# A gated long convolution and an MLP on one core: two causal half-length transforms in a fixed engine order, in place of one padded transform and a scheduled MLP

## The chip, the cores and the metric

The kernel runs on one core of one Trainium2 chip. The metric is device time in microseconds (us), lower is better. TensorE (PE) does the matmuls, VectorE (DVE) and ScalarE (ACT) move accumulated sums out of PSUM (below: evictions) and do the elementwise work, GpSimd (POOL) does small vector work, and SyncE (SP) issues most DMAs. A run has a state: the profiled ones here are fast unless it is said otherwise, and only fast runs enter a ratio.

## The reference, cut to what matters

The sizes are S=2048 positions, D=512 channels and F=1792 hidden channels, in bfloat16.

```python
h  = x + q' * (conv(kv, ssm_k) + kv * ssm_D)     # x = A_q, q' = layernorm(x)
     # kv = (4-tap shift convolution of k) * v
     # conv: rfft over 4096 points (zero padded), product, irfft, first 2048 kept
h2 = h + mlp(layernorm(h))                       # the output
     # g  = gelu(layernorm(.) @ w1); channel quarters shifted by -1, +1, -2, +2 positions
     # x1 = . + g @ w2
     # x1 + gelu(layernorm(x1) @ w3) @ w4
```

The convolution is causal: output half 1 (positions 1024 to 2047) needs input half 1, but output half 0 doesn't. The MLP needs only a few neighbouring positions. So the MLP of half 0 could begin before the convolution of half 1 is done.

## The kernel before

One padded 4096-point transform is written as matmuls in two steps with an exchange by DMA between them. This is done for the filter and for kv. Then come the spectrum products, two inverse steps with a second exchange between them, and then the MLP. Filter and k are brought into their layouts on the chip:

```python
nc.sync.dma_start(hnat[:, c, :], A_ssm_k[c * P:(c + 1) * P, :])
nc.sync.dma_start_transpose(kT[:, c, 16:KW], k_r[:, c * P:(c + 1) * P])
...
nc.tensor.transpose(pt[:, j, :], hnat[:, c, 8 * bh + j:S:16], ident[:])   # 64 of these
...
def step2(z, kh, name):                       # 32 groups of 4 matmuls, 128 x 64
    for r in range(2):
        for t in range(2):
            nc.tensor.matmul(ps[64 * t:64 * t + 64, r, :], lhsT=ftab[:, kh, r, t, :], rhs=z[:, kh, t, :], ...)
...
for i in range(NH + 2):                       # products and inverse, whole sequence
    if i < NH:
        prs[i] = fwd(i)                       # step 2 of kv, eviction on ACT, 2 products on DVE
    if i >= 2:
        inv(i - 2, prs[i - 2])                # 8 matmuls, eviction, DMA exchange
...
plan = Plan({"mm": 6, "pt": 2, "lb": 6, "z": 4})   # from here on: gating, norms and MLP, put in
...                                                # order by a priority search when the kernel is built
for b in range(NB):
    task(("Y", b), {"A": 0.72}, gate(b), ...)
    task(("H", b), {"V": 1.6}, hsum(b), ...)
```

The list of tasks that the search may interleave begins only behind the whole convolution, with the last inverse step.

## Time and profile before

| | before |
|---|---|
| time, median of 3 runs (range) | 268.09 us (267.1 to 268.8) |
| span of the profiled run | 266.8 us |
| PE, DVE, ACT, POOL busy | 231.9, 161.9, 143.3, 54.1 us |
| first w3 matmul | 157 us |

These lines of the page give busy time by engine, and the span in 40 slices of 6.7 us. A digit is the busy share of a slice in tenths, and PEclk is the granted TensorE clock in tenths.

```profile
PE 231.9 (87%) x1803; PEld 119.0 (45%) x1803; DVE 161.9 (61%) x323; ACT 143.3 (54%) x202; POOL 54.1 (20%) x101
...
PE   8665957999579988665988999999999999999994
...
DVE  7986807669927998299999994898022250013322
...
PEclk9999995999959999796899999999999999999999
...
PE 57%; DVE 24%; DMA 6%; ACT 5%; POOL 4%; issue 2%; ACTq 0%; POOLq 0%
```

PE is busy for 87% of the span, but its digits of 9 stand together only from slice 22 on (slices are counted from 0; this one begins at 147 us). Before it they lie between 5 and 9. The last line is the chain of work that ended last, by engine: DVE and DMA hold 30% of it, and that is where PE had to wait.

The same kernel by stage follows: the window, its length, busy time of each engine (with the number of instructions), granted clock, DMA share, GB/s.

```profile
0.00:60.00 60.00, 46.57 (x548) 28.67 (x549) 40.38 (x79) 32.68 (x36) 8.35 (x28) 0.94 0.75 246
60.00:109.00 49.00, 39.74 (x361) 15.71 (x360) 39.69 (x63) 40.43 (x47) 5.59 (x6) 0.93 0.39 143
109.00:152.00 43.00, 34.72 (x332) 22.00 (x332) 36.80 (x91) 29.10 (x51) 28.67 (x49) 0.89 0.27 96
152.00:262.00 110.00, 109.50 (x562) 52.16 (x560) 44.31 (x90) 41.09 (x70) 11.49 (x19) 1.00 0.05 17
```

The columns of busy time are PE, PE weight load, DVE, ACT, POOL. In the last 110 us PE is full and DVE stands at 44. In the first 109 us PE is busy 79% of the time, DVE 73% and ACT 67%: none is full. The limits come one after the other. This piece of the chain of waits (start, length, what) shows the turn at 109 us:

```profile
105.58 3.46 DMA ra<-vst
109.09 3.30 PE mm L549 x31
112.54 0.70 ACT z L560
113.26 0.76 DVE rd L571
114.05 0.70 DVE st L566
114.78 0.18 DVE hv L567
114.96 0.65 DVE rd L571
```

After the exchange and the last inverse step the chain is DVE, block by block: gating (`rd`), statistics (`st`). This is work that PE could have covered, had it had anything else that was ready.

### The profile page before, as it was taken

The page shows a single profiled execution, that of the slowest core. Times are in us where ns is not written, and L with a number is a line of the kernel's source. Part 1 is how long each engine was busy: PE and PEld are TensorE (multiplying, and loading weights), DVE is VectorE, ACT ScalarE, POOL GpSimd, SP SyncE. Part 2 cuts the span into 40 slices and gives each one's busy share as a digit, 9 for nine tenths or more (in the row PEclk, how much of TensorE's full clock was granted, in tenths as well). Part 3 has the DMA queues.
Part 4 walks back from the last instruction along what each step waited for, and adds up shares of the span by engine and source line. Part 5 has one row for each costly group of instructions (what it writes and reads, how often), then busy time and mean ns, then how long its engine had stood idle before and what let it go on. Part 6 is the DMA issues. An engine that isn't in the chain of part 4 may idle for free.

```text
span 266.8 us, 4530 instructions
## 1 busy us (share of the span) xinstructions
PE 231.9 (87%) x1803; PEld 119.0 (45%) x1803; DVE 161.9 (61%) x323; ACT 143.3 (54%) x202; POOL 54.1 (20%) x101
## 2 busy tenths in 40 slices
PE   8665957999579988665988999999999999999994
PEld 3522834555242222224655756445444444444441
DVE  7986807669927998299999994898022250013322
ACT  3638152788479998266867856556500046632000
POOL 3503000000130102029998442251000000000000
PEclk9999995999959999796899999999999999999999
DMA  7999990340701465891000000000011110000111
GB/s 241 249 271 360 407 346 37 142 160 15 295 11 41 153 241 179 295 396 39 1 2 0 4 0 0 2 1 0 2 39 39 39 39 2 0 20 20 42 39 39
DMA packets 18791, 28.08 MB, mean 105 GB/s; under 512 B 10065, under 2 KB 13906, under 8 KB 17234
## 3 DMA queue, kind: packets, MB, share of 16 engines
q1 hardware_dynamic: 17952, 26.74, 29.0%
q0 software_dynamic: 288, 1.05, 1.3%
q8 instruction: 14, 0.23, 0.4%
q10 hardware_dynamic: 530, 0.01, 0.1%
q14 instruction: 7, 0.06, 0.1%
HBM read 11.02 MB, written 2.10 MB: 49 GB/s over the span
## 4 chain that ended last, share of the span: by engine, by line
PE 57%; DVE 24%; DMA 6%; ACT 5%; POOL 4%; issue 2%; ACTq 0%; POOLq 0%
PE mm L717 18%; PE mm L702 18%; DVE st L566 4%; PE pk L406 4%; PE mm L662 3%; DVE rd L571 3%; DMA q_sb<-in_A_q_dram 3%; DMA rd<-rc 2%; DVE rt L315 2%; PE psg L396 2%; DVE vst L342 2%; ACT rc L339 2%; PE psk L396 2%; PE psva L484 2%; DVE pr L474 1%
## 5 line engine op out<-in xcount | busy, mean ns | idle before, releaser
L708 ACT ACTIVATE ra<-mm 128x512 bf16<-128x512 f32 x56 | 33.4, 597 | 49.7 <-PE mm L702 49.6
L702 PE MATMUL mm<-rc,rb 128*128 128x512 bf16 x224 | 50.8, 379 | 0.0
L717 PE MATMUL mm<-rt,ra 128*128 128x512 bf16 x224 | 49.0, 379 | 0.0
L725 DVE TENSOR_TENSOR ob<-mm,rd 128x512 bf16<-128x512 f32 x16 | 11.1, 692 | 61.4 <-PE mm L717 61.4
L717 PEld LDWEIGHTS <-ra 128*128 128x128 bf16 x224 | 22.0, 98 | 26.4
L702 PEld LDWEIGHTS <-rb 128*128 128x128 bf16 x224 | 21.6, 98 | 24.8
L406 PE MATMUL pk<-diag,rb 128*128 128x128 bf16 x256 | 19.8, 238 | 4.4 <-DVE xk L409 4.3
L406 PEld LDWEIGHTS <-rb 128*128 128x128 bf16 x256 | 18.3, 150 | 8.8 <-issue 7.5
L637 PE MATMUL mm<-rc,rf 128*128 128x256 bf16 x128 | 17.8, 295 | 0.0
L530 ACT COPY rc<-ptx 128x512 bf16<-128x512 bf16 x26 | 14.6, 583 | 4.6 <-PE ptx L623 4.6
L662 PE MATMUL mm<-rf,rb 128*128 128x512 bf16 x64 | 16.2, 380 | 1.0 <-ACT rb L643 0.9
L339 ACT CAST asb<-psk 128x1024 bf16<-128x1024 f32 x16 | 16.1, 1030 | 0.5 <-ACT asb L339 0.4
L571 DVE SCALAR_TENSOR_TENSOR rd<-q_sb,qmv,z 128x512 bf16<-128x512 bf16 x16 | 12.7, 792 | 4.6 <-ACT z L560 4.6
L414 DVE BATCH_NORM_STATS2 qst<-q_sb 128x6 f32<-128x512 bf16 x16 | 10.9, 680 | 6.5 <-DMA q_sb<-in_A_q_dram 6.5
L409 DVE TENSOR_TENSOR xk<-pk,rb 128x512 bf16<-128x512 f32 x16 | 10.9, 681 | 6.3 <-PE pk L406 6.2
L560 ACT ACTIVATE z<-mm,qrs 128x512 f32<-128x512 f32 x16 | 10.6, 697 | 7.4 <-PE mm L549 5.7
L637 PEld LDWEIGHTS <-rf 128*128 128x128 bf16 x128 | 13.2, 106 | 2.3
L667 DVE SCALAR_TENSOR_TENSOR q_sb<-rd,cr,mm 128x512 bf16<-128x512 bf16 x16 | 11.7, 733 | 3.7 <-PE mm L662 3.7
L396 PE MATMUL psg<-rd,rf 128*64 128x512 bf16 x64 | 10.3, 418 | 4.2 <-ACT rd L339 4.0
L396 PEld LDWEIGHTS <-rf 128*64 128x64 bf16 x128 | 5.7, 115 | 17.2 <-issue 16.2
L473 DVE TENSOR_TENSOR pr<-asb,rd 128x1024 bf16<-128x1024 bf16 x16 | 11.0, 687 | 3.5 <-ACT asb L339 3.5
L339 ACT CAST rd<-psg 128x1024 bf16<-128x1024 f32 x13 | 13.0, 1028 | 0.0
(224 smaller groups left out, 347.2 us busy)
## 6 DMA issues: line engine op xcount, KB each, us to landing
rd<-rc SPq DMA_DIRECT2D x16, 256.0 KB, 6.0
rc<-ra SPq DMA_DIRECT2D x16, 256.0 KB, 2.4
ra<-vst SPq DMA_DIRECT2D x16, 256.0 KB, 2.4
ra<-in_A_ssm_k_dram SPq DMA_DIRECT2D x4, 512.0 KB, 5.1
rb<-in_A_v_dram SPq DMA_DIRECT2D x2, 1024.0 KB, 8.0
q_sb<-in_A_q_dram SPq DMA_DIRECT2D x2, 1024.0 KB, 8.3
out_dram<-ob SPq DMA_DIRECT2D x16, 128.0 KB, 1.8
rb<-in_B_w_dram SPq DMA_DIRECT2D x1, 1792.0 KB, 7.3
```

Source lines behind the costliest of these rows:

```text
L339: nc.scalar.copy(o, i)
L396: nc.tensor.matmul(ps[64 * t:64 * t + 64, r, :], lhsT=ftab[:, kh, r, t, :], rhs=z[:, kh, t, :], start=True, stop=True)
L406: nc.tensor.matmul(pk[:, c * P:(c + 1) * P], lhsT=kT[:, c, 16 + b - j:KW - 16 + b - j + 1:16], rhs=diag[:, c, j, :], start=(j == 0), stop= ...
L530: nc.scalar.copy(o, i)
L571: nc.vector.scalar_tensor_tensor(out=h_sb[:, b, :], in0=q_sb[:, b, :], scalar=qmv[:, b, 0:1], in1=tl["z", b][:], op0=SUB, op1=MUL)
L637: nc.tensor.matmul(pw_[:, j * 256:(j + 1) * 256], lhsT=w1_sb[:, k, m * P:(m + 1) * P], rhs=hnT[:, k, p * 256:(p + 1) * 256], start=(k == 0 ...
L662: nc.tensor.matmul(px[:], lhsT=shifted(m, b), rhs=w2_sb[:, m, :], start=(m == 0), stop=(m == DC - 1))
L667: nc.vector.scalar_tensor_tensor(out=x1[:, b, :], in0=hbm[:, b, :], scalar=tl["cr", b // 2][:, b % 2:b % 2 + 1], in1=tl["x", b][:], op0=MU ...
L702: nc.tensor.matmul(pg[:], lhsT=w3_sb[:, k, fc * P:(fc + 1) * P], rhs=lnT[:, k, g * 512:(g + 1) * 512], start=(k == 0), stop=(k == DC - 1))
L708: nc.scalar.activation(gbuf[:, g % 2, fc, :], tl["g", g, fc][:], ACT.Gelu_apprx_tanh)
L717: nc.tensor.matmul(po[:], lhsT=gbuf[:, g % 2, fc, i * P:(i + 1) * P], rhs=w4_sb[:, fc, :], start=(fc == 0), stop=(fc == FC - 1))
L725: nc.vector.tensor_tensor(out=ob[:], in0=tl["o", 4 * g + i][:], in1=xh1[:, b, :], op=ADD)
```

## The change

Its intent is to do the convolution as two causal halves, so that the MLP of half 0 covers the convolution of half 1. The diff replaces nearly the whole file. Its core, cut:

```diff
-    def __init__(self, pools, rounds=40):
-        best = self.solve()      # the search, at build time, for what follows the convolution
+ORDER = """
+005S 023V 004S 011S 021P7 022P 056P01 003S 030V 031G 006S 054P23 055V 001A 058P45 ...
+""" # 791 words for ALL work: task number, engine letter, slots. Every engine runs its tasks in this order.
...
-            nc.tensor.matmul(ps[64 * t:64 * t + 64, r, :], lhsT=ftab[:, kh, r, t, :], rhs=z[:, kh, t, :], ...)
+    for h in range(4):       # 64x32 tiles, 16 matmuls in a group, 16 groups
+        nc.tensor.matmul(ps[32 * h:32 * h + 32, sl[2 * t + r], :], lhsT=ftab[64 * t:64 * t + 64, 4 * kl + h, r, :],
+                         rhs=z2[sig][64 * t:64 * t + 64, kl, h, :], start=True, stop=True)
...
+    conv(0, [("A0", "F0")])                       # half 0: one product of spectra
+    conv(1, [("A0", "F1"), ("A1", "F0")])         # half 1: two
...
+    add(("P", s, kl, i, x, t), {V: 0.605, GP: 2.4}, ...)   # 5 of the 48 products stand on GpSimd in ORDER
+    add(("XI", s, kl, t), {SP: 0.5}, ...)         # exchange for the inverse: all DMAs on SyncE
+    add("Lsk", {A: 0.5}, lambda e, s: nc.scalar.dma_start(ssk[:], sk), size=1)   # the 4 KB tap table
...
-                nc.tensor.transpose(pt[:, c, :], tl[key][:, c * P:(c + 1) * P], ident[:])
+    BYDMA = {("hb", 0, 2), ("hb", 0, 3), ("hb", 1, 1), ...}       # 12 of 16 pairs of blocks:
+    nc.sync.dma_start(d[...], src(...))                            # to DRAM and, transposed, back
+    nc.sync.dma_start_transpose(dst(sl[0])..., d[:]...)
...
+    fx = a["A_ssm_k"].T.reshape(...)              # filter, k and weights laid out on the host
```

F0, F1 are the filter halves and A0, A1 those of kv. Table angles are worked out partly on GpSimd.

## The prediction

> **What bounds the kernel now.** The page gives busy times PE 232, DVE 162, ACT 143, POOL 54 of 266.8 us, but the limits follow one another (windowed table, chain of waits). To 109 us runs the convolution: the chain alternates between PE, evictions on DVE and ACT, and DMA (scatter 6 us, q load 7 us); a table build on DVE costs 5.7. From 109 to 152 us, layer norm and gating: the chain is almost all DVE (0.65 + 0.70 and small ones for each block) and PE runs about 15.6 of 20 us at a granted clock of 0.83. From 152 to 263.5 us PE is continuously busy, with DVE and ACT mostly idle.
>
> **What the change does.**
> 1. Less PE work. Two inputs come transposed from the host: 64 PE transposes (5.4 us) and four DMA transposes go, as do 62 table matmuls (4 us). The halves replace 32 step-2 groups (0.55 each, 17.6) by 16; as 64x32 tiles I cost a group at 0.43 to 0.55. The inverse becomes 24 groups of 0.43 to 0.55 (10 to 13) for 16 of 0.97 (15.5). Step 1 stays near 17. The shift goes from 16 x 1.15 to 16 x 0.93. 96 of 128 layer-norm transposes (0.055 each) go to DMA: 5 us. The four MLP matmuls stay near 125. New PE sum: 187 to 193 us.
>    The small groups hold 16 matmuls, one every 27 ns. The Trainium skill ("TensorE: Matmul & The Clock Gate", "Wait — 56ns, not 53.3ns?") gives a floor near 25 ns; here 32 table matmuls with their weight loads started within 0.75 us, 24 ns each: it agrees. The skill's "TensorEngine Tiling" (Key Properties) says that a change of tiling mode drains the array; here a step-2 group takes 0.55 instead of 0.43 when it alternates. About 56 changes: an estimated 6 us.
> 2. DVE and ACT work hardly changes: 80 evictions of 1024 columns before and after (1.02 ACT, 1.15 DVE); 48 products of 0.60 to 0.69 for 32, five on POOL; 18 statistics move from DVE to ACT. I expect DVE 150 to 165, ACT 130 to 145.
> 3. Overlap, the real aim. The second half's convolution runs beside the first half's MLP. In the new order DVE has about 82 us of work ahead of the first w3 matmul and PE 66; behind it PE has 120 and DVE about 60. So the first 90 to 95 us stay bound by evictions, products and loads, the rest by PE.
>
> **Sum.** 90 to 94 us to the first w3 matmul (before: 157), 120 us of PE, 2 to 4 of hiccups, 4 of last sum and store: 215 us. The removed PE work counts only in part, since early PE waited anyway; overlap gives most of the 50 us.
>
> **Predicted 215 us, 8 in 10 between 205 and 229.** Faster by over 2%: 0.97; within 2%: 0.02; slower: 0.01.
>
> **What would show it.** PE busy near 190 us, 87% of the span; DVE and ACT unchanged within 10 us; first w3 matmul at 85 to 98 us; PE digits of 9 from there on; PE idle mostly before 60 us, released by evictions, products and DMA; DMA transposes landing in 3 to 7 us, hardly ever what PE waits for.
>
> **What would make it wrong.** A fixed order cannot adapt: one late DMA or POOL product (2 to 3 us) blocks an engine. Small-tile weight loads might not overlap (up to +10 us). DMA transpose round trips with two buffers might stall PE late. Early PE idleness may hold the clock down.

## The result, and the profile after

The changed kernel ran at 233.66 us (median of 4 runs, 232.47 to 235.62). Before's 4 runs had a median of 268.44 (267.1 to 269.45). The ratio is 0.8731, with a 95% interval of 0.8673 to 0.8788: faster by 12.7%, but 4.7 us outside the predicted range. Ratios here and below are from fast runs alone; they are not quite the ratio of the medians.

| | before | predicted | after |
|---|---|---|---|
| span of the profiled run | 266.8 | | 230.7 |
| first w3 matmul | 157 | 90 to 94 | 103.7 |
| from there to the start of the last w4 matmul | | 122 to 124 | 122.9 |
| PE busy | 231.9 | near 190 | 204.2 |
| DVE, ACT busy | 161.9, 143.3 | 150 to 165, 130 to 145 | 156.4, 131.6 |

The same lines of the page as before (slices are now 5.8 us):

```profile
PE 204.2 (89%) x2040; PEld 116.8 (51%) x2040; DVE 156.4 (68%) x402; ACT 131.6 (57%) x203; POOL 63.2 (27%) x114
...
PE   7589768799385898799979999999999999999993
...
DVE  7599989999289998989968971838785344100331
...
PEclk9999979999889599999999999999999999999999
...
PE 59%; DMA 15%; DVE 13%; ACT 5%; issue 4%; SPq 2%; DVEq 0%
```

DVE went from 24% of the chain to 13%, DMA from 6% to 15%, and a new name, SyncE's queue (SPq), has come in. In slice 10 (from 57.7 us) PE has a 3 and DVE a 2. In slice 13 (from 75.0 us) the clock is at 5. The stages (same columns):

```profile
0.00:60.00 60.00, 47.26 (x648) 20.93 (x648) 53.07 (x104) 43.52 (x51) 24.34 (x73) 0.97 0.80 275
60.00:80.00 20.00, 14.53 (x179) 5.54 (x180) 15.49 (x51) 15.34 (x22) 8.13 (x10) 0.79 0.85 301
80.00:104.00 24.00, 21.19 (x330) 11.37 (x329) 21.46 (x55) 20.25 (x32) 8.33 (x6) 0.96 0.52 142
104.00:227.00 123.00, 121.21 (x887) 78.99 (x885) 65.72 (x193) 52.54 (x102) 22.43 (x26) 1.00 0.30 68
```

Up to 104 us DVE is busy 90.0 us and PE 83.0; neither is full. From there PE is full at full clock. So the whole surprise is in the front. The chain of waits shows its pieces:

```profile
3.63 6.67 DMA ssk<-in_sk_dram
...
52.11 1.94 ACT r_vs L259 x2
54.06 0.57 SPq L484
...
55.45 1.38 SPq L402
...
58.20 0.59 SPq L484
...
58.89 6.03 DMA r_v<-in_w_dram
...
65.20 1.04 PE ps L492 x8
...
86.58 3.26 DMA hnT<-dhb
...
94.49 3.03 DMA hnT<-dhb
```

Three suspects stand there. The 4 KB table of shift taps, issued while the big loads run, holds 6.67 us of the chain. At 50 to 59 us SyncE issues a backlog of twelve DMAs, some 0.6 us each: in its one order the filter's exchange (L402) and the inverse exchange (L484) alternate, and it had stood still for 5.2 us from 44.5, at an L402 whose data was late. The last inverse exchange then travels beside those L402 transfers and the w1 and w2 loads until 65 us (the chain writes the name of the transfer that landed last). Two DMA transposes cost 3.3 and 3.0 us. A fourth suspect is in the timeline: GpSimd's products beside DVE's.

```profile
32.39 2.12 POOL L463 TENSOR_TENSOR r_p<-r_a,r_f 128x1024 bf16<-128x1024 bf16 x1 [14.22 <-ACT r_a L259]
32.54 3.13 DVE L463 TENSOR_TENSOR r_p<-r_a,r_f 128x1024 bf16<-128x1024 bf16 x2
39.67 3.23 DVE L463 TENSOR_TENSOR r_p<-r_a,r_f 128x1024 bf16<-128x1024 bf16 x2
39.85 2.49 POOL L463 TENSOR_TENSOR r_p<-r_a,r_f 128x1024 bf16<-128x1024 bf16 x1 [5.34 <-DMA r_v<-in_v_dram]
```

Two products on DVE take 1.4 us elsewhere (686 ns each for the 16 that write from `r_x`); beside a GpSimd product they took 3.13 and 3.23. The Trainium skill ("SBUF — State Buffer", Who interferes with whom) says that a DVE instruction with two SBUF inputs contends with a GpSimd instruction that reads SBUF, for a port pair that is locked and not shared out. This trace agrees: DVE lost about 1.8 us each time, near the length of the GpSimd product. The skill ("GPSIMD Engine Reference", 4.1 Engine selection) puts two-input operations on GpSimd at about twice VectorE's time; here the mean is 2306 ns against 686, 3.4 times, waits for the lock included.

### The profile page after: what moved, and what is told of

Its sections match the earlier page's. It is cut to its first block, busy times and chain, and to the rows that moved or that the text cites. A ratio compares the mean times of both kernels' runs of the same rounds, so it can differ in the third digit from the quotient of the medians.

```text
span 230.7 us, 5231 instructions
## 1 busy us (share of the span) xinstructions
PE 204.2 (89%) x2040; PEld 116.8 (51%) x2040; DVE 156.4 (68%) x402; ACT 131.6 (57%) x203; POOL 63.2 (27%) x114
## 4 chain that ended last, share of the span: by engine, by line
PE 59%; DMA 15%; DVE 13%; ACT 5%; issue 4%; SPq 2%; DVEq 0%
PE ps L743 20%; PE ps L730 20%; PE ps L683 5%; DMA hnT<-dhb 4%; PE ps L654 3%; PE ps L473 3%; DMA ssk<-in_sk_dram 3%; DVE r_kv L439 3%; DMA r_v<-in_w_dram 3%; DMA dhb<-hbt 3%; PE ps L387 2%; PE ps L492 2%; PE ps L410 2%; DVE r_y L259 2%; DMA r_a<-r_y 2%
## 5 line engine op out<-in xcount | busy, mean ns | idle before, releaser
L730 PE MATMUL ps<-r_dg,r_k 128*128 128x256 bf16 x448 | 51.4, 273 | 0.0
L730 PEld LDWEIGHTS <-r_k 128*128 128x128 bf16 x448 | 43.5, 98 | 8.4 <-issue 1.2
L734 ACT ACTIVATE r_x<-ps 128x512 bf16<-128x512 f32 x35 | 19.3, 599 | 24.8 <-PE ps L730 24.8
L743 PE MATMUL ps<-w4s,r_x 128*128 128x512 bf16 x140 | 31.5, 379 | 0.0
L463 DVE TENSOR_TENSOR r_p<-r_a,r_f 128x1024 bf16<-128x1024 bf16 x27 | 21.1, 824 | 1.1 <-PE ps L473 1.0
L259 ACT CAST r_y<-ps 128x1024 bf16<-128x1024 f32 x20 | 19.3, 1018 | 4.0 <-DMA r_f<-r_y 2.1
L463 POOL TENSOR_TENSOR r_p<-r_a,r_f 128x1024 bf16<-128x1024 bf16 x5 | 11.5, 2306 | 29.3 <-ACT r_a L259 14.2
L431 PE MATMUL ps<-r_dg,r_k 128*128 128x256 bf16 (+3 forms) x112 | 16.4, 298 | 2.9 <-DVE r_dg L305 1.8
L743 PE MATMUL ps<-w4s,r_kv 128*128 128x512 bf16 x84 | 18.8, 379 | 0.0
L654 PE MATMUL ps<-hnT,r_v 128*128 128x256 bf16 x128 | 16.2, 282 | 2.8 <-DMA hnT<-dhb 2.6
L654 PEld LDWEIGHTS <-r_v 128*128 128x128 bf16 x128 | 12.7, 101 | 6.6 <-DMA hnT<-dhb 3.8
L431 PEld LDWEIGHTS <-r_k 128*128 128x128 bf16 x112 | 9.7, 100 | 11.6 <-issue 7.5
L683 PE MATMUL ps<-r_v,r_h 128*128 128x512 bf16 x64 | 15.3, 380 | 0.0
```

The lines of the kernel that those rows point to most:

```text
L259: (act.copy if e == A else vec.tensor_copy)(o, i)
L431: nc.tensor.matmul(o[:, (d + j0) * P:(d + j1 + 1) * P], lhsT=kT[:, s, c, bb, x:x + P], rhs=diag[:, c, j0:j1 + 1, :].rearrange("p j x -> p ...
L463: on[e].tensor_tensor(out=prs[:, sl[0], :, :], in0=sp[a][:, kl, t, :, :], in1=gv, op=MUL)
L654: nc.tensor.matmul(ps[:, sl[0], j * 256:(j + 1) * 256], lhsT=w1s[:, k, m * P:(m + 1) * P], rhs=hnT[:, k_, k, :], start=(k == 0), stop=(k = ...
L683: nc.tensor.matmul(ps[:, sl[0], :], lhsT=h1T[:, m, bb, x:x + P], rhs=w2s[:, m, :], start=(m == 0), stop=(m == DC - 1))
L730: nc.tensor.matmul(ps[:, sl[0], j * 256:(j + 1) * 256], lhsT=w3s[:, k, fc * P:(fc + 1) * P], rhs=lnT[:, k_, k, :], start=(k == 0), stop=(k ...
```

## The experiments

Eighteen kernels were run. The first theory: the front is the sum of DVE's work and a few blockages in the fixed order, so lifting a blockage gains what the chain shows for it. Its rival: DVE isn't the pace; many waits lie side by side (landing of the exchanges, table and weight loads, small PE groups at a lowered clock), and lifting one uncovers the next. A third question is what the overlap itself is worth. The expectations use letters in their own way: B mostly stands for DVE as the pace, A for late transfers, queue order and the rest, C for a late start, D for the DMA transposes.

In the variants ORDER was broken into lines anew, so line numbers are 10 higher than in the changed kernel. One word of ORDER is a task: 135G2 is task 135 on GpSimd with slot 2.

| run | time, us | ratio to before [95%] | first w3, us | clock 0 to 100 us |
|---|---|---|---|---|
| changed kernel | 233.66 | 0.8731 [0.8673, 0.8788] | 103.7 | 0.93 |
| c0_same (control) | 234.44 | 0.8777 [0.8739, 0.8815] | 105.2 | 0.90 |
| c0_again (control) | 233.30 | 0.8776 [0.8727, 0.8825] | 103.9 | 0.93 |
| a1_nopool | 231.13 | 0.8647 [0.8609, 0.8686] | 101.2 | 0.91 |
| a3_ssk | 233.62 | 0.8722 [0.8682, 0.8763] | 102.2 | 0.93 |
| a8_xiact | 230.60 | 0.8626 [0.8590, 0.8662] | 101.1 | 0.95 |
| d1_three | 230.49 | 0.8614 [0.8575, 0.8654] | 101.6 | 0.95 |
| a4_flip | 235.12 | 0.8800 [0.8766, 0.8834] | 106.2 | 0.91 |
| a2_w4early | 233.79 | 0.8748 [0.8703, 0.8792] | 104.5 | 0.90 |
| a2_w4late | 239.41 | 0.8962 [0.8916, 0.9009] | 111.5 | 0.86 |
| d4_three_w4early | 231.32 | 0.8647 [0.8613, 0.8680] | 101.3 | 0.95 |
| d2_all | 231.85 | 0.8653 [0.8607, 0.8699] | 100.1 | 0.95 |
| e2_qlate | 230.18 | 0.8642 [0.8602, 0.8682] | 100.3 | 0.95 |
| g1_best | 233.93 | 0.8765 [0.8716, 0.8814] | 104.9 | 0.90 |
| e1_noload2 (wrong) | 240.18 | 0.9012 [0.8964, 0.9061] | 109.5 | 0.88 |
| e3_noload2_alone (wrong) | 234.14 | 0.8764 [0.8713, 0.8815] | 105.3 | 0.88 |
| f1_lightdve (wrong) | 231.63 | 0.8662 [0.8613, 0.8712] | (slow) | (slow) |
| a6_nooverlap | 264.63 | 0.9929 [0.9884, 0.9974] | 138.4 | |
| b1_layout (from before) | 263.91 | 0.9872 [0.9823, 0.9921] | | |

The last two columns come from one profile each. f1's profiled run counted as slow, so it has no entry there. The ratios have intervals of about 0.4 points either way, and many of them come from different calls. One percentage point of the ratio is 2.7 us.

### Controls: c0_same and c0_again

The edit is line breaks in ORDER alone.

> The changed kernel itself, with its order list only broken into other lines: the control for this chip. All theories: 0.873 of the time before, first w3 matmul near 104 us, span near 231 us. If it falls outside 0.867 to 0.879, differences of one per cent between runs of different calls can't be read.

> The control again, for this call: 0.873 to 0.878 of the time before, first w3 matmul at 104 to 105 us.

Both agree with the changed kernel (0.5 points away, with overlapping intervals), and with each other to 0.01 points. Single profiles of one and the same program put the first w3 matmul at 103.7, 105.2 and 103.9 us, so a difference of 1.5 us there means nothing.

### What is the overlap worth? a6_nooverlap

```diff
-... 348V 173P76 353V 356V 332S 354V 333S 370V 230P01 358G0 ...
+... 348V 173P76 353V 356V 332S 354V 333S 230P01 358G0 ...   (370V and all tasks behind the
+                  convolution and the first half's gating come after the last convolution task)
```

> The same tasks on the same engines in two phases: first both convolution halves (with the first half's last inverse and gating), then everything of the MLP, each phase in the old relative order. This undoes the overlap of the second half's convolution with the first half's MLP. If the overlap earns most of the gain, as I predicted: the MLP's 120 us of PE start only when all of the convolution is done, and the time rises by 15 us or more, to over 245. If the overlap earns little, because DVE and ACT set the pace early and MLP work only stretches the convolution: convolution done near 90 us, first w3 matmul at 105 to 115, w4 at once behind, total 225 to 236.

The time was 264.63 us, 0.9929 of before. The page of this run:

```profile
PE   7398577984957767536769899999999999999994
...
PEclk9889999997775555558799999999999999999999
```

and its stages (same columns as above):

```profile
60.00:80.00 20.00, 14.27 (x164) 4.07 (x165) 12.98 (x28) 14.52 (x19) 3.82 (x5) 0.73 0.78 280
80.00:100.00 20.00, 14.02 (x209) 4.51 (x205) 11.56 (x19) 12.07 (x17) 4.74 (x2) 0.50 0.42 140
100.00:120.00 20.00, 11.76 (x121) 4.94 (x121) 17.02 (x51) 3.85 (x4) 7.89 (x7) 0.50 0.21 53
```

Without the MLP between them, the small transform groups don't keep PE busy, the granted clock falls to 0.50 for 40 us, and each inverse matmul takes 545 ns in the mean where it took 381. In 80 to 100 us no engine is busy more than 14 of 20 us: the work goes round from PE to ACT to DVE and back. The Trainium skill ("TensorE: Matmul & The Clock Gate", Part 1, What's actually happening) says that the clock is gated to one half when PE has been idle; the 0.50 agrees. But idle has to be read widely: the trace has the clock at one half from 76.0 to 120.4 us, and from 64 to 109 us no pause of PE was longer than 2.0 us. So the overlap gives 11.5 points (0.9929 less the control's 0.8777), about 31 us, which is nearly the whole gain; all the rest of the change, in this two-phase order, gave 0.7 points. The 31 us are an upper bound in one sense: this is one two-phase order made by hand, not the best one. How they split between filled gaps and clock was not measured.

### How much is the host layout worth? b1_layout

The edit is to the kernel before: k and the filter arrive transposed, the 64 PE transposes with their evictions and the four DMA transposes go.

```diff
-        nc.sync.dma_start_transpose(kT[:, c, 16:KW], k_r[:, c * P:(c + 1) * P])
+        nc.sync.dma_start(kT[:, c, 16:KW], A_k[c * P:(c + 1) * P, :])
-                nc.tensor.transpose(pt[:, j, :], hnat[:, c, 8 * bh + j:S:16], ident[:])
+    (filter loaded straight into xh, in four DMAs)
```

> The kernel before with one part of the change: k and the long filter come transposed from the host, so its 64 PE transposes with their 8 evictions and its four DMA transposes go; all else stays. If host layout is a large part of the gain: 5 to 9 us less (the chain had 0.7 us of these transposes, 0.6 us of their evictions and DMA waits of 6 and 7 us behind a queue that the transposes filled for 26 us). If the early stage is held by the table build on DVE (5.7 us) and by the other loads: under 3 us.

It gained 1.3 points, about 3.4 us of before's 267, within 2%. Taking work off PE where PE waits gains little.

### The GpSimd products: a1_nopool

```diff
-... 135G2 ... 145G2 ... 297G1 ... 299G2 ... 313G0 ...
+... 135V2 ... 145V2 ... 297V1 ... 299V2 ... 313V0 ...
```

> The five spectrum products that run on GpSimd go to DVE, nothing else. Theory A (the first 104 us are late because transfers land late): DVE gets 5 x 0.6 = 3 us more work, waits for DMA stay; the first w3 matmul moves by less than 1 us and the time by less than 0.5%. Theory B (DVE itself is slower than I costed, because a GpSimd product holds up a DVE product: two of them took 2.4 and 2.6 us instead of 0.6): mean of a DVE product falls from 0.82 to 0.69 us, busy DVE stays within 1 us of 156, the first w3 matmul comes 1 to 3 us earlier.

The gain was 1.3 points (3.5 us). DVE's busy time did not grow by five products; it fell from 156.5 to 154.9 us. The five products on GpSimd cost DVE more in blocked time than they relieved it of work.

### The tap table: a3_ssk

```diff
-    add("Lsk", {A: 0.5}, lambda e, s: nc.scalar.dma_start(ssk[:], sk), size=1)
+    add("Lsk", {A: 0.5}, lambda e, s: nc.sync.dma_start(ssk[:], sk), size=1)     # first of all in the order
```

> The 4 KB shift-filter load (and the 1 KB one) are issued first on SyncE instead of on ScalarE behind its first activation. In the changed kernel it was issued at 3.6 us and landed at 10.3 us; DVE waited 2.4 us for it. Theory C (the start is late): it lands by 4 us, the diagonal tables are built from about 8 us, everything after moves 2 us earlier, time down by 1.5 to 2.5 us. Theory A and B: what is won at the start is lost again before 60 us, because the transfers or the DVE work in between set the pace; under 0.7 us.

The table landed 1.6 us after its issue and left the chain of waits. But the shift matmuls began at 11.1 instead of 11.4 us: in this order they stand behind the filter's step-1 groups and their evictions, and the chain now runs through those (PE from 10.12 us, the shift from 11.16). The ratio fell by 0.5 points (1.5 us) with overlapping intervals: unclear. Six microseconds of the chain were worth a fraction of that, because another wait of nearly the same length lay beside it.

### The inverse exchange issued elsewhere: a8_xiact

```diff
-    nc.sync.dma_start(wv[s][4 * t + kl:P:8, :, :, :], vst[...])
+    (nc.sync if s else nc.scalar).dma_start(wv[s][4 * t + kl:P:8, :, :, :], vst[...])   # right behind its evictions
```

> The eight inverse transfers of the first half are issued by ScalarE right after the evictions they wait for, instead of standing in SyncE's one order between the second filter's transfers. Theory A: SyncE no longer waits on those evictions, so the F1 transfers go out from 50 us at once, the first F1 step 2 starts before 60 us (was 61.7), the first last-inverse matmul at 61 to 63 us (was 65.2); first w3 matmul 2 to 4 us earlier, time down 2 to 4 us. If it is bandwidth and not order (DMA engines 92 to 94% busy from 50 to 70 us): last-inverse start stays within 1 us of 65. Theory B: no change over 1 us.

The gain was 1.5 points (4.0 us). The last inverse step began at 63.1 us (control 65.0), and the clock around it was higher. These are the last issues in front of it, first the control's, then those of this run (start, length, what; L412 is the filter's exchange, L494 the inverse one):

```profile
54.99 1.94 SPq L412 DMA_DIRECT2D r_f<-r_y  x2
57.05 1.21 SPq L494 DMA_DIRECT2D r_x<-r_vs  x2
```

```profile
44.22 10.03 SPq L412 DMA_DIRECT2D r_f<-r_y  x8
58.06 1.19 ACTq L494 DMA_DIRECT2D r_x<-r_vs  x2
...
58.63 4.37 DMA r_x<-r_vs
```

The inverse exchange was not issued earlier: its last issue came at 58.63 us, in the control at 57.66. But it landed after 4.37 us and not after 7.04. What went out earlier is the filter's exchange (last issue at 53.65 us, control 56.33): from 50 us on, it no longer had four inverse issues of about 0.6 us between its own. And the w1 and w2 loads came 2 us later (60.44, control 58.45). Which of these, or the ring of its own, made the landing faster was not separated.

The windows after it, the control's and then that of this run (columns as in the stages above):

```profile
60.00:80.00 20.00, 14.20 (x168) 4.62 (x168) 14.20 (x43) 13.40 (x18) 7.80 (x10) 0.73 0.77 275
```

```profile
60.00:80.00 20.00, 15.28 (x224) 6.40 (x231) 17.92 (x58) 18.34 (x25) 9.14 (x11) 0.91 0.90 328
```

The same 20 us held 224 recorded matmuls, not 168. In the control PE paused for 3.7 us from 57.7 us, and the granted clock stood at one half from 62.3 to 69.1; here no pause in that stretch was longer than 1.2 us and the clock stayed full until 74.0. Such a hole is thus paid for twice in these profiles, in waiting and in a slow clock afterwards. How much of the gain is the clock isn't shown: against the three profiles of the control the last inverse step began 1.9 to 2.9 us earlier, the first w3 matmul 2.6 to 4.1 us. The Trainium skill ("DMA: Bandwidth & Descriptors", Issuing engines are not separate DMA queues) says that issuing from a second engine saves only the sequencer's issue time. This run doesn't contradict that, but that time was not small here: four issues of 0.6 us in a backlog are most of the 2.7 us by which the filter's exchange went out earlier.

### All three together: d1_three, and more loads moved: a2_w4early, d4_three_w4early, d2_all, e2_qlate

```diff
 d1_three:          a1_nopool + a3_ssk + a8_xiact
 a2_w4early:        control, w4 load (334S) moved up to 34 us
 d4_three_w4early:  d1_three + a2_w4early
 d2_all:            d4 + w3 load early, three q statistics (421V 423V 426V) late
 e2_qlate:          d1 + q load of the second half behind w4, three q statistics late
```

> The three edits that each helped, together: no products on GpSimd (3.5 us faster than the control, by the ratios), shift filter first on SyncE (1.5), first half's inverse transfers issued by ScalarE (4.0). If the three losses lie one behind the other on the path to the first w3 matmul: they add, 8 to 9.5 us, time near 225 us, first w3 matmul at 95 to 97 us, which is where the prediction put its late end, and 123 to 124 us from there to the last w4 matmul as in all runs so far. If they hide each other (each only uncovers the next wait): less than 6 us, time over 228.

> The control with the w4 load moved to 34 us, behind the last input load, where SyncE idles for 8 us and the DMA engines go to 37% busy. Moved late it cost 5 us, because the two small writes for a DMA transpose stood 6.1 us behind 3.5 MB of weights. If that reading is right, moved early it takes nothing from the transposes (first w1 to first w2 matmul 13 us as in the control or less, not 18), and leaves less traffic beside the last inverse transfers: time equal or up to 1.5 us less. If it delays the first transfers of the long filter's second half: last-inverse start later than 65 us, time up to 2 us more.

> d1_three and the early w4 load together: what a2_w4early gains or loses on top of d1_three, within 1 us; 223 to 227 us if early helps.

> d4 with, besides, three statistics of the second half's q (0.8 us of DVE each) put behind the first w3 matmuls, and the w3 load put right behind those of w1 and w2 instead of behind the second half's transfers. If DVE sets the pace in the front, the statistics give up to 2.4 us; if weights beside transfers cost, the w3 load at 62 us gives back some of it on the transfers of A1. Between 1.5 us slower and 2.5 us faster than d4.

> Correct: d1_three with the second half's q (1 MB, issued at 32.0 us) loaded behind w4, and its three early statistics put behind the first w3 matmuls. If transfers before 40 us are the limit, 1 MB less (3 us at 340 GB/s) gives 1 to 2.5 us: time 228 to 229.5. If not, within 0.7 us of d1_three.

The gains don't add up. Apart they were 3.5, 1.5 and 4.0 us, together 4.3 us (0.8777 less 0.8614). The chain of waits of d1_three shows what took the place of the tap table:

```profile
11.58 6.42 DMA r_v<-in_v_dram
...
57.96 5.22 DMA r_x<-r_vs
```

The early w4 load gained nothing for certain. e2_qlate began its last inverse step at 59.8 us, 3.5 us ahead of d1_three, but its first w3 matmul only 1.3 us ahead, and its time is the same: the lead was given back.

### Loads at a bad moment: a2_w4late, g1_best

```diff
 a2_w4late:  -... 333S 370V 230P01 358G0 334S ... 246S 335S 274V3 ...
             +... 333S 370V 230P01 358G0 ...      246S 335S 334S 274V3 ...      (w4 right behind w3)
 g1_best:    d1 + w4 at 34 us + second q load behind w3 (335S 020S), q statistics late
```

> The 1.75 MB load of w4 leaves its place (issued at 60.7 us, behind w1 and w2 and ahead of the second half's first transfers) and goes behind that of w3 (76.8 us). It is needed at 125 us. Theory A, bandwidth: the last two inverse transfers landed 6.6 us after issue beside the weight loads, earlier ones alone in 3.3; without w4 they land 1 to 2 us earlier and so does everything behind them; time down 1 to 2 us. Theory A, order only, and theory B: the transfers stand ahead of the weights in the same queue, so nothing moves; within 0.5 us.

> Correct: d1_three with the w4 load at 34 us, clear of the inverse transfers, and the second half's q behind the w3 load, its three early statistics behind the first w3 matmuls. The inverse transfers then share the engines only with w1 and w2. Best guess from the landmarks: first last-inverse matmul at 60 us (e2_qlate), then 38 us to the first w3 matmul, time 227.5 to 229.5; if the stretches hide each other again, 230 to 231.

a2_w4late lost 1.9 points (5 us). Its chain has the cause:

```profile
87.22 6.14 DMA dhb<-hbt
```

The small write that starts a DMA transpose took 6.14 us behind 3.5 MB of weights in the same queue; in the three profiles of the control the same write took 2.4 to 2.7 us from issue to landing. From the first w1 to the first w2 matmul it was 18.4 us, in the control 13.1. g1_best put another load of 1 MB at the same place (17.5 us there) and lost what d1 had gained. The name was given before the run; it isn't the best.

### Is it the DMA transposes? a4_flip

```diff
-    BYDMA = {("hb", 0, 2), ("hb", 0, 3), ("hb", 1, 1), ...
+    BYDMA = {("hb", 1, 1), ...       # these two pairs by PE transposes and evictions
```

> Blocks 4 to 7 of the first half are transposed for w1 by PE (with an eviction of 0.4 to 0.6 us each) and not by two DMA round trips. In the changed kernel the chain waits 3.3 and 3.0 us for these transposes at 87 and 95 us. Theory D (the round trip through DRAM holds up the front): w1 of these blocks starts 3 to 5 us earlier, first w3 matmul 2 to 4 us earlier, time down 1 to 3 us. If PE would have waited for products and evictions anyway (theory B): first w3 matmul within 1 us, time within 0.5%, or slower, for DVE and ACT get 2 us more.

The time is that of the control (0.88). The two DMA transposes held 6.3 us of the chain, but without them the first w3 matmul came no earlier (106.2 us): other waits took their place (a DMA wait of 6.08 us from 78.2 us now stands on the chain), and PE, DVE and ACT had the transposes and evictions to do.

### Is it the amount of early loads? e1_noload2, e3_noload2_alone

The second half's filter, k and v are never loaded, which takes away 3080 KB. Their outputs are wrong, which doesn't matter for the times.

```diff
 e3_noload2_alone:  control -  load(("Lf", 1), ...)  load(("Lk", 1, c), ...)  load(("Lv", 1, g), ...)
 e1_noload2:        d1_three - the same loads
```

> Wrong on purpose: d1_three, but the second half's filter, k and v are never loaded, the first half's tiles are read in their place; all instructions on PE, DVE, ACT and GpSimd stay. 3.06 MB less to load in the first 40 us. If the transfers of the first 40 us are the limit underneath: the exchanges of A0 land 3 us or more earlier, the first last-inverse matmul at 56 to 60 us (63.3 in d1_three), first w3 matmul at 94 to 98 us (101.6), time 223 to 227 us. If DVE and ACT set the pace: last-inverse start within 2 us of 63, time within 1.5 us of d1_three's 230.5.

> Wrong on purpose: the same loads taken away from the changed kernel itself, without the three edits. If the transfers are the limit: a gain of 2 to 5 us alone, less than on top of the three edits, for the GpSimd products and the one order of SyncE still hold. If not: within 1 us of the control.

e3 is equal to the control: in this order the amount of early traffic isn't the limit. e1 did the unexpected. With less to load it lost 4.0 points against d1_three, some 10 us. Its chain (start, length, what) has this line:

```profile
57.26 12.52 DMA r_x<-r_vs
```

The inverse exchange landed 12.52 us after its issue, where d1_three had 5.22. With the loads gone, SyncE came to the w4 load at 54.3 us, so that it ran on SyncE's ring at the same time as the exchange on ScalarE's ring:

```profile
w4s<-in_w_dram SPq DMA_DIRECT2D x1, 1792.0 KB, 15.2
...
r_x<-r_vs ACTq DMA_DIRECT2D x4, 256.0 KB, 11.0
```

From 60 to 66 us the trace shows 86 packets of 4096 bytes starting on ScalarE's ring and 104 of 14,336 bytes on SyncE's (from 62 to 64 us 33 and 34). The Trainium skill ("DMA: Bandwidth & Descriptors", Queues, rings and completion order) says that a DMA engine goes round between queues packet by packet; the trace agrees, nearly. So the ring with packets 3.5 times as long took about four times as many bytes, and the urgent exchange got the small share. In d1_three only w1 and w2 ran beside it. The last inverse step began at 69.8 us, 6.5 us behind d1_three. This cause is read from one profile of each run: no run moved the w4 load in e1 alone.

### Is it DVE's work? f1_lightdve

This one, too, is wrong on purpose: products of the second half over half the columns, q statistics over 64 columns.

```diff
+    w = D // 2 if s else D
-    on[e].tensor_tensor(out=prs[:, sl[0], :, :], in0=sp[a][:, kl, t, :, :], in1=gv, op=MUL)
+    on[e].tensor_tensor(out=prs[:, sl[0], :, 0:w], in0=sp[a][:, kl, t, :, 0:w], in1=gv[:, :, 0:w], op=MUL)
-    x = q_sb[:, s, b, :]
+    x = q_sb[:, s, b, 0:64]
```

> Wrong on purpose: the changed kernel with the second half's spectrum products over half of their columns (0.35 us instead of 0.6 on DVE, the GpSimd ones halved too) and the statistics of q over 64 columns instead of 512 (about 0.2 instead of 0.68 us); same instructions, order and waits. If DVE sets the pace of the front (theory B): from the first last-inverse to the first w3 matmul 31 to 35 us (39 to 40 in the controls), and the first last-inverse matmul 2 to 5 us before 65; time 6 to 11 us less than the control's 233 to 234. If transfers, PE order and ACT set it (theory A): each stretch within 2 us of the control, time at most 3 us less.

DVE's busy time fell by 15 us, from 156.5 to 141.6 (f1's slow profile), some 10 of them in the first 104 us. The fast runs gained 1.1 points, 3 us, which is less than a1_nopool gained by giving DVE more products. GpSimd's products were halved too, so even these 3 us are not all DVE throughput. The first theory's main term falls here: 10 us of DVE's work in the front were worth at most 3, so DVE's work alone doesn't set its length.

## Why the prediction was right or wrong

**Right: the direction, and the cause of the gain.** "Overlap, the real aim": a6_nooverlap takes it away and 11.5 of the 12.2 points go.

**Right: the late part.** "120 us of PE, 2 to 4 of hiccups, 4 of last sum and store": from the first w3 matmul to the start of the last w4 matmul 122.9 us, then 4.1 us to the end of the span. In the correct variants with the overlap it was 122.3 to 124.5 us wherever the front ended. PE digits are 9 from there on with a single 7.

**Right: totals of DVE and ACT** (156.4 and 131.6 us), and the named risks that a GpSimd product blocks an engine (a1_nopool, 3.5 us) and that early PE idleness holds the clock down (0.79 in 60 to 80 us).

**Wrong: the step "90 to 94 us to the first w3 matmul".** It measured 103.7 us. Of the 18.7 us between 215 and 233.66 this step is 11.7, taken from 92. Another 4 us is an error of the sum itself: its terms add up to 216 to 222 us, middle 219, and 215 was written beneath them. About 3 us lie between the profiled span (230.7) and the median device time: 1.8 from the span to its own run (232.47), as in the runs of the kernel before (263.3 and 265.11), which was not allowed for, and 1.2 because that run was the fastest of the four. The late terms were right and add nothing.

The front failed in two ways. Its terms were too small: DVE had 90 us of work there, not 82, and PE 83, not 66 (step 1 alone has 320 matmuls against 256 before, and was reckoned as "near 17" where the groups show 22.1 us; part of PE's busy is modelled ends and slow clock). And the rule was wrong: the length was taken as the work of the fullest engine plus a start. f1_lightdve took 15 us of DVE's work away, 10 of them in the front, and gained 3, e3_noload2_alone took 3 MB of loads away and gained nothing, a4_flip took the two transposes off the chain and gained nothing. What moved the front was when transfers landed and what stood ahead of them or beside them (a8_xiact 4.0 us one way, a2_w4late 5 us and e1_noload2 10 us the other), and GpSimd blocking DVE (a1_nopool, 3.5 us).

**Wrong in part: "DMA transposes landing in 3 to 7 us, hardly ever what PE waits for".** They (`hnT`) landed in 2.9 to 3.1 us, but are 4.0% of the chain of waits; a4_flip took away the two in the front, and that gained nothing.

**Not tested: "a change of tiling mode drains the array", an estimated 6 us.** No run isolates it. Step-2 groups of 16 took between 0.56 and 1.10 us in the chain, at different clocks.

**Still open.** The three blockages together give 4.3 us, and no run came below 100.1 us to the first w3 matmul. The remaining 6 to 10 us against the predicted front are, as I read it, hand-overs from PE to an eviction to DVE to a DMA in a fixed order, and a clock that falls in their gaps. The table fits: every profile with a clock of 0.95 over the first 100 us has its first w3 matmul by 101.6 us, and of those at 0.91 and below all but a1_nopool come after 104. Around 58 us a pause of PE comes first and the half clock after it (a8_xiact), but for the front as a whole no run decides which is cause and which is effect, and the low clock (0.88) of e3's profile may hide a gain. Nor did any run make ACT's evictions or PE's small groups lighter, so they stay rivals. This is argued, not shown.

**A version that beats both.** d1_three, a8_xiact, e2_qlate and a1_nopool (230.2 to 231.1 us) are correct and 1.3 to 1.6 points below the changed kernel's controls. Their intervals don't touch the controls', but the difference is under 2%. They can't be told apart from one another. a8_xiact is the smallest edit to the DMAs; a1_nopool changes five letters.

## What to carry to other kernels

Where no engine is full, neither the sum of the fullest engine's work nor the lengths on the chain of waits tell what a stage will cost or what a lifted wait will gain: pieces of 6 to 7 us on the chain were worth 4 us, 1.5 (not clear of noise) and nothing here, so each has to be tried. In a fixed order, look for a backlog of issues on one engine, and for bulk loads that share the DMA engines with a small urgent transfer; where they stood was worth 4 to 10 us, more than any removal of work in the front. Here the overlap of two independent halves was worth more than all the rest of the change (11.5 of 12.2 points); without it PE was less busy and its clock fell too.

## What the Trainium skill lacked or had wrong

- "DMA: Bandwidth & Descriptors" (Queues, rings and completion order) states the turns packet by packet but not what follows for a short urgent transfer: beside a load in packets of 14,336 bytes, an exchange in packets of 4096 bytes landed after 12.52 us; beside w1 and w2 alone it took 5.22 us.
- The same page (Issuing engines are not separate DMA queues) calls the issue time that a second issuing engine saves usually small. Here one issue took about 0.6 us, but twelve stood in one backlog from 49.8 to 58.8 us, and moving eight DMAs to ScalarE gained 4.0 us.
- No section that I looked up gives what a small write costs behind bulk loads in one queue: 6.14 us behind 3.5 MB, against 2.4 to 2.7 us in the control.
- "GPSIMD Engine Reference" (4.1 Engine selection) gives about 2 times VectorE's time for two-input operations; the bf16 products of 128 x 1024 took 2306 ns against 686 ns, 3.4 times, waits for the shared ports included. The split was a loss here: five products moved back to DVE lowered DVE's busy time by 1.6 us.
